# Zero rows under small float32 products, and other rules in the planner that orders the kernel

## The chip, the cores and the metric

One core of a Trainium2 chip runs the whole program in one launch. The metric is the device time of one execution in microseconds (us). A change of about one per cent is the least that a measurement of this kernel can tell from none.

## The reference

Three parts follow each other: a gated recurrence with a matrix state (4 batches, 8 heads, 768 steps, 40 features), then two feed-forward layers on its output (3072 rows of 320).

```python
for t in range(S):
    m_new = np.maximum(f_gate[:, :, t] + m, i_gate[:, :, t])
    f_stab = np.exp(f_gate[:, :, t] + m - m_new)
    i_stab = np.exp(i_gate[:, :, t] - m_new)
    C = f_stab[:, :, None, None] * C + i_stab[:, :, None, None] * np.einsum('bhd,bhe->bhde', vt, kt)
    n = f_stab[:, :, None] * n + i_stab[:, :, None] * kt
    h_tilde = np.einsum('bhde,bhe->bhd', C, qt)
    denom = np.maximum(np.abs(np.einsum('bhd,bhd->bh', n, qt)[:, :, None]), 1.0)
    y[:, :, t] = 1.0 / (1.0 + np.exp(-o_gate[:, :, t])) * h_tilde / denom
...
h = x @ w_in;  x = np.maximum(0.01 * h, h) @ w_out      # layer 0, 320 -> 2048 -> 320
h = np.maximum(x @ w_in, 0.0);  out = h * h @ w_out     # layer 1
```

## The kernel before

The recurrence is done in six chunks of 128 steps. Inside a chunk it has the form of attention: for each of eight groups g (four heads of one batch) the scores of keys and queries (`mS`, line 644, into PSUM tile `attS`), times a decay mask `aw`, times the values (`mPV`, line 660, or `mPV3`, line 666, into `atty`), plus queries times the carried state (`mI`, line 654). The state update is `mU` (line 721), for two batches at a time into `attm`; the outcome is transposed by `mT` (line 763) into `xH` and `xL`, the two halves of the number that the layers multiply. `gate_T` (lines 555, 556) turns the gates of a chunk, `bc` (line 624) spreads them over the partitions in chunk 0.

The first two chunks (`c < NATIVE`) use plain float32 products: their keys and queries lie 40 partitions high in `raw` (tiles `w8` to `w15` in chunk 0, `X` in chunk 1), and the state `C32` is 40 partitions high too. Later chunks stack three copies to 120 partitions (tiles `T`, `Cst`).

Layer 0 and layer 1 split each weight into a high and a low part (`weight`, lines 395 to 421, on VectorE, ScalarE and GpSimd); `moe_h` (line 442) makes a hidden block in `hp` with eight matmuls, `out1` (lines 473 to 479) and `out2` (lines 522 to 524) sum them up in the tiles `acc`. For the first chunk half blocks of 256 columns are used, so that the layer can begin before the whole chunk is there.

No instruction is issued in the order of the code. Each is a `Node` with an engine, an assumed duration in ns, a `key` and what it reads and writes; `Sched.order` runs a planner: `forward` walks through time and gives each free engine the ready node with the least key, `backward` gives each node the latest start that would still do as its next key, six passes, and the shortest plan is issued word for word. When TensorE would have nothing to do, early in the plan, a product of zeros is put in (`sc.idle`; lines 330, 469 and 487, tile `warm`); none of its results is used. A node with `alt` may go to GpSimd in place of VectorE. All transfers are issued on SyncE's queue, in the plan's order. ScalarE's instructions also wait in a row: a change between the tables of Exp and Sigmoid loads a table (ACT_TABLE_LOAD).

Of the kernel before, what the change touches and what calls it, by code (L numbers as in the profile page):

```python
# [19 lines left out]
E = 42  # L20
CH = 128
# [12 lines left out]
PASSES = 6  # L34
WARM = 18500
# [12 lines left out]
class Node:  # L48
    __slots__ = ("eng", "dur", "fn", "key", "deps", "outs", "ndep", "ready", "allocs", "bufs", "end", "start", "table", "lat", "seq", "alt", "after", "first", "bank", "small")


class Sched:
# [10 lines left out]
    def op(self, eng, dur, key, fn, r=(), w=(), table=None, lat=0, alt=None, after=0, small=False):  # L63
# [5 lines left out]
        n.seq, n.outs, n.allocs, n.end = len(self.nodes), [], [], None  # L69
        deps, bufs = {}, {}  # L70
# [25 lines left out]
    def order(self, passes):  # L96


        import copy

        best = None
        for i in range(passes):
            try:
                plan, total = self.forward()
            except RuntimeError:
                if best is None:
                    raise
                break
            if best is None or total < best[1]:
                best = [copy.copy(n) for n in plan], total  # L110
            self.backward(plan, total)
        return best[0]

    def backward(self, plan, total):
# [4 lines left out]
        lst, g = {}, [(-1e9, total)]  # L119
        for n in sorted((n for n in plan if n.seq >= 0), key=lambda n: (n.start, n.seq), reverse=True):  # L120
# [7 lines left out]
            t -= 2000 + n.lat if n.lat else 0  # L128
            if n.eng == "PE":
                i = next(i for i, (lo, hi) in enumerate(g) if min(hi, t) - lo >= n.dur)  # L130
                lo, hi = g[i]
                t = min(hi, t)
                g[i:i + 1] = [x for x in ((t, hi), (lo, t - n.dur)) if x[1] - x[0] > 60]
# [4 lines left out]
    def forward(self):  # L138
        import heapq

# [22 lines left out]
        out, now, dma_free, done, last, small = [], 0.0, 0.0, 0, 0.0, False  # L163
        while done < len(self.nodes):

            for e, cand in ready.items():
# [3 lines left out]
                for n in sorted(cand, key=lambda n: (n.key, n.seq)):  # L170
                    if all(b.live or (b.first is n and queue[b.tag][-1] is b and free[b.tag] > 0) for b in n.bufs):
# [4 lines left out]
                        if e != "PE" or pick.small or not small or n.key > pick.key + STAY:  # L176
                            break
                if pick is None:
                    if e == "PE" and self.idle and (now < 12000 or now - last > 300) and (fill := next((f for f in self.idle if f[1].live and f[2].start is None), None)):
# [4 lines left out]
                        busy[e] = n  # L184
                        heapq.heappush(at, (now + n.dur, 0, -1))
                    continue
                n = pick
                if n.alt:
                    other = n.alt[0] if e == n.eng else n.eng
                    if e != n.eng:  # L190
                        b = busy[other]
                        ahead = (b.start + b.dur - now if b else 0) + sum(x.dur for x in ready[other] if (x.key, x.seq) < (n.key, n.seq) and x.eng == other)
# [3 lines left out]
                    ready[other].remove(n)  # L196
                cand.remove(n)
# [17 lines left out]
                busy[e] = n  # L215
                heapq.heappush(at, (now + dur, 0, n.seq))
                end = now + dur
                if n.lat:
                    begin = max(end + 1300, dma_free)
                    dma_free = begin + n.lat * (1.5 if begin < 13000 else 1.1)  # L220
                    end = dma_free + 700
                n.end = end
# [13 lines left out]
            elif what == 1:  # L236
                ready[n.eng].append(n)
                if n.alt:
                    ready[n.alt[0]].append(n)
# [31 lines left out]
def mlstm_moe_kernel(  # L271
# [40 lines left out]
    C32 = fixed([D, B * H, E], name="C32")  # L312
    Cst = fixed([3 * D, B * H, E], F32R, name="Cst")
    fi, am = sb("x2_0", [32, 2, S]), sb("x2_1", [32, 2, S])
# [19 lines left out]
    def consts():  # L334
        V.memset(mt.t[:, 0:1], NEG)
        V.memset(am.t[:, 1], 1.0)
        V.memset(am.t[:, 1].rearrange("p (k t) -> p k t", t=CH)[:, :, 0:1], 0.0)

    op("DVE", 900, -300, consts, w=[(mt, 0), (am, "mask")])
    op("POOL", 800, -300, lambda: make_identity(nc, ident.t), w=[(ident, 0)])  # L340

    GP = [0, CH, 2 * CH, S]

    def gate_part(lo, hi, key):
# [6 lines left out]
        a = lambda: am.t[:, 0, o]  # L351
# [9 lines left out]
        def clamp():  # L361
            V.tensor_scalar(out=a(), in0=a(), scalar1=AMIN, scalar2=None, op0=ALU.max)
            if lo == 0:
                V.memset(am.t[:, 0, 0:1], 0.0)
# [507 lines left out]
```

## Time and profile before

| | us |
|---|---|
| median of 3 runs | 856.56 |
| lowest and highest | 851.53, 859.89 |
| the profiled execution, its own time | 853.73 |
| its span, first to last instruction | 851.0 |
| mean granted TensorE clock in it | 0.989 |

The profiled execution has 2.73 us outside its span. Its clock is given as a share of 2.4 GHz; 0.50 is 1.2 GHz.

### The profile page before, as it was taken

The page shows a single profiled execution, that of the slowest core. Times are in us where ns is not written, and L with a number is a line of the kernel's source. Part 1 is how long each engine was busy: PE and PEld are TensorE (multiplying, and loading weights), DVE is VectorE, ACT ScalarE, POOL GpSimd, SP SyncE. Part 2 cuts the span into 40 slices and gives each one's busy share as a digit, 9 for nine tenths or more (in the row PEclk, how much of TensorE's full clock was granted, in tenths as well). Part 3 has the DMA queues.
Part 4 walks back from the last instruction along what each step waited for, and adds up shares of the span by engine and source line. Part 5 has one row for each costly group of instructions (what it writes and reads, how often), then busy time and mean ns, then how long its engine had stood idle before and what let it go on. Part 6 is the DMA issues. An engine that isn't in the chain of part 4 may idle for free.

```text
span 851.0 us, 13708 instructions
## 1 busy us (share of the span) xinstructions
PE 836.9 (98%) x5159; PEld 720.7 (85%) x5162; DVE 528.3 (62%) x967; ACT 464.1 (55%) x928; POOL 98.8 (12%) x133
## 2 busy tenths in 40 slices
PE   9899999999999999999999999999999999999998
PEld 6799888788878878887888889999999999999997
DVE  6999955766776786666657898353443533533433
ACT  6678566657766775786455675343433433433332
POOL 2475440202011120001000000000000000000000
PEclk9999989999999999999999999999999999999999
DMA  7677352435344353543322441000000000000000
GB/s 221 225 270 223 99 145 89 138 113 167 109 136 149 127 165 113 167 132 95 99 69 94 146 136 68 1 32 1 1 32 0 24 9 1 32 1 1 32 1 31
DMA packets 52210, 78.58 MB, mean 92 GB/s; under 512 B 4336, under 2 KB 40784, under 8 KB 52144
## 3 DMA queue, kind: packets, MB, share of 16 engines
q1 hardware_dynamic: 52144, 77.71, 28.8%
q8 instruction: 40, 0.66, 0.3%
q14 instruction: 26, 0.21, 0.1%
HBM read 54.26 MB, written 4.01 MB: 68 GB/s over the span
## 4 chain that ended last, share of the span: by engine, by line
PE 75%; DVE 9%; DMA 5%; ACT 4%; SPq 3%; issue 2%; POOL 0%; DVEq 0%; ACTq 0%
PE hp L442 33%; PE acc L473 4%; PE acc L524 3%; PE acc L523 3%; PE acc L522 3%; PE acc L475 3%; PE acc L474 3%; DMA aw<-Adram 3%; SPq L590 3%; PE attS L644 2%; PE acc L478 2%; PE acc L479 2%; PE atty L654 1%; PE atty L524 1%; PE atty L522 1%
## 5 line engine op out<-in xcount | busy, mean ns | idle before, releaser
L442 PE MATMUL hp<-xH,w 128*128 128x512 f32 (+1 forms) x995 | 289.5, 388 | 0.0
L442 PEld LDWEIGHTS hp<-xH,w 128*128 128x128 f32 x995 | 179.4, 189 | 29.8
L442 PE MATMUL hp<-xL,w 128*128 128x512 f32 (+1 forms) x597 | 196.4, 384 | 0.6 <-DVE xL L769 0.6
L454 DVE TENSOR_TENSOR g<-g 128x512 f32<-128x512 f32 x96 | 66.4, 691 | 118.7 <-ACT g L453 118.7
L442 PEld LDWEIGHTS hp<-xL,w 128*128 128x128 f32 x597 | 111.6, 189 | 24.1 <-DVE xL L769 0.8
L453 ACT ACTIVATE g<-hp 128x512 f32<-128x512 f32 x96 | 57.3, 597 | 129.5 <-PE hp L442 129.4
L456 DVE TENSOR_TENSOR gL<-g,gH 128x512 fp32r<-128x512 f32 x96 | 66.4, 692 | 56.4 <-ACT gH L455 56.4
L455 ACT CAST gH<-g 128x512 fp32r<-128x512 f32 x96 | 59.5, 620 | 68.8 <-DVE g L454 68.8
L448 ACT ACTIVATE gH<-hp 128x512 fp32r<-128x512 f32 (+1 forms) x103 | 58.3, 566 | 51.0 <-PE hp L442 46.3
L450 DVE TENSOR_TENSOR gL<-hp,gH 128x512 fp32r<-128x512 f32 (+1 forms) x103 | 66.9, 650 | 30.7 <-ACT hp L449 30.1
L473 PE MATMUL acc<-gH,w 128*128 128x512 f32 (+1 forms) x206 | 82.7, 402 | 0.0
L475 PE MATMUL acc<-gL,w 128*128 128x512 f32 (+1 forms) x206 | 78.3, 380 | 0.0
L474 PE MATMUL acc<-gH,w 128*128 128x512 f32 (+1 forms) x206 | 78.1, 379 | 0.0
L524 PE MATMUL acc<-w,gL 128*128 128x320 f32 x192 | 59.3, 309 | 0.0
L523 PE MATMUL acc<-w,gH 128*128 128x320 f32 x192 | 59.3, 309 | 0.0
L522 PE MATMUL acc<-w,gH 128*128 128x320 f32 x192 | 59.2, 308 | 0.0
L449 ACT ACTIVATE hp<-hp 128x512 f32<-128x512 f32 (+1 forms) x103 | 57.7, 560 | 0.0
L638 POOL TENSOR_SCALAR_AFFINE_SELECT aw<-aw 128x512 f32<-128x512 f32 x48 | 33.6, 701 | 201.6 <-ACT aw L635 172.3
L635 ACT ACTIVATE aw<-aw,cs 128x128 f32<-128x128 f32 x160 | 50.7, 391 | 6.6 <-DMA aw<-Adram 6.3
L475 PEld LDWEIGHTS acc<-gL,w 128*128 128x128 f32 x206 | 39.3, 191 | 7.7 <-DVE gL L450 0.2
L473 PEld LDWEIGHTS acc<-gH,w 128*128 128x128 f32 x206 | 39.6, 192 | 6.3
L474 PEld LDWEIGHTS acc<-gH,w 128*128 128x128 f32 x206 | 39.4, 191 | 5.7
(160 smaller groups left out, 1432.7 us busy)
## 6 DMA issues: line engine op xcount, KB each, us to landing
T<-X SPq DMA_DIRECT2D x144, 120.0 KB
x<-in_wts_dram SPq DMA_DIRECT2D x16, 704.0 KB
aw<-Adram SPq DMA_DIRECT2D x40, 256.0 KB
nat<-in_nat_dram SPq DMA_DIRECT2D x24, 328.0 KB
qkr<-in_qk_dram SPq DMA_DIRECT2D x16, 360.0 KB
X<-in_wts_dram SPq DMA_DIRECT2D x8, 704.0 KB
T<-in_wts_dram SPq DMA_DIRECT2D x8, 704.0 KB
og<-in_og_dram SPq DMA_DIRECT2D x12, 320.0 KB
```

What stands on the lines that cost most here:

```text
L442: T.matmul(hp.t[:, 0:n], w.t[:, col:col + 128], x.t[:, kt, o], start=(s == 0), stop=(s == 7))
L448: op("ACT", act(n, True), key, lambda: A.activation(gH.t[:, 0:n], h(), AF.Prelu, alpha=0.01), r=[(hp, 0)], w=[(gH, 0)])
L450: op("DVE", dve(n), key, lambda: V.tensor_tensor(out=gL.t[:, 0:n], in0=h(), in1=gH.t[:, 0:n].bitcast(F32), op=ALU.subtract), r=[(hp, 0), ( ...
L454: op("DVE", dve(n), key, lambda: V.tensor_tensor(out=g.t, in0=g.t, in1=g.t, op=ALU.mult), r=[(g, 0)], w=[(g, 0)])
L455: op("ACT", act(n), key, lambda: A.copy(gH.t, g.t), r=[(g, 0)], w=[(gH, 0)])
L456: op("DVE", dve(n), key, lambda: V.tensor_tensor(out=gL.t, in0=g.t, in1=gH.t.bitcast(F32), op=ALU.subtract), r=[(g, 0), (gH, 0)], w=[(gL, 0)])
L473: T.matmul(a[t].t[:, o], w.t[:, hc:hc + 128], gH.t[:, 0:n], start=first, stop=False)
L474: T.matmul(a[t].t[:, o], w.t[:, lc:lc + 128], gH.t[:, 0:n], start=False, stop=False)
L475: T.matmul(a[t].t[:, o], w.t[:, hc:hc + 128], gL.t[:, 0:n], start=False, stop=last)
L522: T.matmul(a.t[:, 0:DM], gH.t[:, s], wH, start=first, stop=False)
L523: T.matmul(a.t[:, 0:DM], gH.t[:, s], wL, start=False, stop=False)
L524: T.matmul(a.t[:, 0:DM], gL.t[:, s], wH, start=False, stop=last)
```

## The change

- `pad` writes zeros to partitions 40 to 127 (in two pieces, 64 to 127 and 32 to 63, the transfer or the update writes over 32 to 39 later) of `C32`, of `raw` for groups 4 to 7 in chunk 0, and of `X` once for all of chunk 1. The products `mS` and `mI` of these then run over 128 rows. Groups 0 to 3 of chunk 0 stay at 40 rows. `C32` and `X` are written by ScalarE (four copies), the four tiles of chunk 0 by GpSimd or VectorE (eight memsets).
- Each TensorE node has `act`, the part of its time that counts as activity, weighted by its share of rows. `dense` adds this up over the last `SPAN` of the plan. Where a small product would leave less than `DENSE`, another ready product or a product of zeros goes first.
- A transfer is issued only when fewer than `DEPTH` are in flight in the plan; `backward` places VectorE, ScalarE and the transfers in time too, not TensorE alone; after the six passes 160 rounds change some keys at random and keep what makes the planned time no longer.
- Assumed durations of small products are other numbers (`mS` 248 for 214, `mI` and `mPV` 226, `mU` 850 for 1170, `gate_T` 530 for 380).
- The low part of a weight is made on VectorE by `scalar_tensor_tensor` (times 1, minus) in place of `tensor_tensor`. A second place for products of zeros is opened in chunk 1. The mask of the gates is shorter.

```diff
@@ order
+        rnd = random.Random(3)
+        for i in range(ROUNDS):
+            sigma, mid, half = rnd.choice((300, 1000, 3000)), rnd.uniform(0, 100e3), rnd.choice((5e3, 10e3, 20e3))
+            for n, (k, s) in zip(self.nodes, keys):
+                n.key = k + (rnd.gauss(0, sigma) if abs(s - mid) < half else 0)
...
+            if total <= best[1]:
+                best = [copy.copy(n) for n in plan], total
+                keys = [(n.key, n.start) for n in self.nodes]
@@ backward
-            t -= 2000 + n.lat if n.lat else 0
...
+            if n.lat:
+                t = (place(gaps["DMA"], t - 700, 1.2 * n.lat) if "DMA" in gaps else t - 700) - 1.2 * n.lat - 1300
+            if n.eng in gaps:
+                t = place(gaps[n.eng], t, n.dur)
@@ forward
+        def dense(n):
+            lo = now + n.dur - SPAN
+            while past and past[0][1] <= lo:
+                past.pop(0)
+            return n.act + sum(a * (min(1, (e - lo) / (e - s))) for s, e, a in past) >= DENSE * SPAN
...
+                if e == "PE" and pick is not None and pick.small and 7000 < now and not dense(pick):
+                    other = next((n for _, _, n in cand if not n.small and all(b.live or (b.first is n and queue[b.tag][-1] is b and free[b.tag] > 0) for b in n.bufs)), None)
+                    pick = other or (None if any(f[1].live and f[2].start is None for f in self.idle) else pick)
...
+                if n.lat and len(flight) >= DEPTH:
+                    dur = max(dur, flight[-DEPTH] - now)
@@ the kernel
-    C32 = fixed([D, B * H, E], name="C32")
+    C32 = fixed([128, B * H, E], name="C32")
...
+    def pad(t, buf, n, key, ks, act_=True):
+        for p0, p1 in ((64, 128), (32, 64)):
+            w = [(buf, f"z{p0}")] + (ks if p0 == 32 else [])
+            if act_:
+                op("ACT", act(n), key, lambda p0=p0, p1=p1: A.copy(t()[p0:p1], warm.t[p0:p1, 0:1].to_broadcast([p1 - p0, n])), r=[(warm, 0)], w=w)
+            else:
+                op("POOL", 1.05 * n + 90, key, lambda p0=p0, p1=p1: G.memset(t()[p0:p1], 0.0), w=w, after=5300,
+                   alt=("DVE", dve(n, True), lambda p0=p0, p1=p1: V.memset(t()[p0:p1], 0.0)))
+
+    pad(lambda: C32.t.rearrange("p h e -> p (h e)"), C32, B * H * E, -250, [(C32, (b, k)) for b in range(B) for k in range(2)])
...
+            if eng is V:
+                eng.scalar_tensor_tensor(out=w.t[:, o:o + n], in0=x, scalar=1.0, in1=y, op0=ALU.mult, op1=ALU.subtract)
...
+                    full = c > 0 or g >= 4
+                    if c == 0 or not g:
+                        raw = sb(f"w{(11, 10, 9, 8, 15, 14, 13, 12)[g]}" if c == 0 else "X", [128 if full else D, 2, 4, CH])
+                        if full:
+                            pad(lambda raw=raw: raw.t.rearrange("p a h t -> p (a h t)"), raw, 1024, -240 + g, [(raw, 0)], c > 0)
```

What the change does to the order of instructions is shown at two places. In the rows an operation stands with its line, its tiles and partitions x columns; the line numbers are those of the file that the row is from, and after the change `mS` is line 712, `mI` 722, `mU` 789, `mPV` 728, `mT` 831, `gate_T` 619 and 620, `moe_h` 506, `out1` 537 to 543.

The first is TensorE's row at the last state update of chunk 1 (`mU` into `attm`). Before:

```order
L475 MATMUL acc_235<-gL,w_927 128x512
L721 MATMUL attm<-wv,nat 40x42 x16
L644 MATMUL attS<-X 128x128 x4
L654 MATMUL atty<-C_69,X 128x42 x4
L555 MATMUL attS<-ident,G_sb 128x96
L556 MATMUL attS<-ident,G_sb 128x32
L660 MATMUL atty<-nat,aw 128x42 x4
L478 MATMUL acc_243<-gH,w_927 128x512
```

After:

```order
L728 MATMUL atty<-nat,aw 128x42 x4
L506 MATMUL hp<-xH,w_1039 128x512 x4
L506 MATMUL hp<-xL,w_1039 128x512 x2
L506 MATMUL hp<-xH,w_1039 128x512
L506 MATMUL hp<-xL,w_1039 128x512
L831 MATMUL attm<-ident,y 128x128 x3
L722 MATMUL atty<-C_69,X 128x42 x4
L712 MATMUL attS<-X 128x128 x4
L789 MATMUL attm<-wv,nat 40x42 x16
L728 MATMUL atty<-nat,aw 128x42 x4
L619 MATMUL attS<-ident,G_sb 128x96
L542 MATMUL acc_260<-gH,w_542 128x256
```

The small products still stand in one run here, with a whole hidden block ahead of them; what differs is that the products on `X` and `C32` now have 128 rows each.

The second is ScalarE's row from its start (`og` are the output gates, `d` a one-column tile that only makes a table load early, `cs` and `ex` the turned gates, `aw` the masks of the first groups). Before:

```order
L329 ACT_TABLE_LOAD
L329 ACTIVATE d<-d 128x1
L559 COPY cs<-attS 128x32
L560 ACT_TABLE_LOAD
L560 ACTIVATE ex<-attS 128x96
L635 ACTIVATE aw<-hp,cs 128x128 x4
L635 ACTIVATE aw<-acc_163,cs 128x128 x4
L569 ACT_TABLE_LOAD
L569 ACTIVATE og<-og 128x1280
L635 ACT_TABLE_LOAD
L635 ACTIVATE aw<-acc_194,cs 128x128 x4
```

After:

```order
L395 CAST C_69<-warm 64x1344
L395 CAST C_69<-warm 32x1344
L378 ACT_TABLE_LOAD
L378 ACTIVATE d<-d 128x1
L395 CAST X<-warm 64x1024
L633 ACTIVATE og<-og 128x1280
L395 CAST X<-warm 32x1024
L635 ACT_TABLE_LOAD
L635 ACTIVATE d<-d 128x1
L623 COPY cs<-attS 128x32
L624 ACTIVATE ex<-attS 128x96
L703 ACTIVATE aw<-hp,cs 128x128 x4
```

The four copies of zeros and the Sigmoid of the output gates now stand ahead of the first exponentials, and the table no longer changes between the masks of the first four groups. On SyncE's queue the second part of the gates and the output gates are now issued second and third; before they stood seventh and eighth, behind the first four key and query tiles.

## Rows read from the trace of the kernel before

**Rows 1.** The page, parts 1 and 2: TensorE's busy time, granted clock in 40 slices.

```profile
PE 836.9 (98%) x5159; PEld 720.7 (85%) x5162; DVE 528.3 (62%) x967; ACT 464.1 (55%) x928; POOL 98.8 (12%) x133
...
PEclk9999989999999999999999999999999999999999
```

**Rows 2.** Windows by stage: busy us of each engine, granted clock, DMA share, GB/s.

```profile
0.00:32.38 32.38, 29.52 (x206) 22.09 (x210) 23.31 (x55) 19.21 (x48) 10.26 (x16) 0.95 0.78 236
32.38:105.00 72.62, 70.00 (x561) 62.88 (x561) 70.24 (x127) 52.34 (x121) 42.73 (x54) 0.95 0.60 194
105.00:150.00 45.00, 45.00 (x263) 38.92 (x261) 25.21 (x54) 30.85 (x69) 10.92 (x15) 0.92 0.43 119
150.00:450.00 300.00, 294.65 (x1987) 241.31 (x1987) 204.67 (x424) 195.32 (x412) 34.33 (x48) 1.00 0.40 126
```

**Rows 3.** Windows, the four stretches at the lower clock, columns as in rows 2.

```profile
23.66:27.07 3.41, 3.01 (x33) 2.22 (x35) 2.42 (x8) 0.78 (x2) 0.72 (x1) 0.50 0.82 312
50.96:54.38 3.42, 3.42 (x41) 3.11 (x42) 3.41 (x8) 2.79 (x7) 3.02 (x6) 0.50 0.85 294
78.27:81.68 3.41, 3.41 (x16) 3.31 (x16) 3.30 (x10) 1.75 (x4) 3.25 (x4) 0.50 0.71 176
105.58:112.40 6.82, 6.82 (x28) 6.21 (x28) 4.78 (x11) 5.39 (x16) 5.63 (x8) 0.50 0.29 97
```

**Rows 4.** TensorE's timeline before the fall at 105.58: start, us, instruction, idle before.

```profile
103.39 0.81 PE L721 MATMUL attm<-wv,nat 128*40 128x42 f32 x32 [0.86 <-DVE xL L769]
104.14 1.16 PE L644 MATMUL attS<-X 40*128 40x128 f32 x8
105.13 1.35 PE L654 MATMUL atty<-C,X 40*128 40x42 f32 x8
```

**Rows 5.** TensorE's timeline around small products of 40 and of 128 rows.

```profile
67.87 0.28 PE L474 MATMUL acc<-gH,w 128*128 128x256 f32 x1
67.99 0.28 PE L475 MATMUL acc<-gL,w 128*128 128x256 f32 x1
68.20 1.16 PE L644 MATMUL attS<-X 40*128 40x128 f32 x8
69.19 0.98 PE L654 MATMUL atty<-C,X 40*128 40x42 f32 x8
70.10 0.39 PE L478 MATMUL acc<-gH,w 128*128 128x256 f32 x1
...
71.14 0.98 PE L660 MATMUL atty<-nat,aw 128*128 128x42 f32 x8
71.95 0.47 PE L473 MATMUL acc<-gH,w 128*128 128x512 f32 x1
```

**Rows 6.** ScalarE's timeline at the start.

```profile
8.51 0.19 ACT L559 COPY cs<-attS 128x32 f32<-128x32 f32 x1 [6.22 <-PE attS L556]
8.71 1.28 ACT L560 ACT_TABLE_LOAD   x1
10.01 0.25 ACT L560 ACTIVATE ex<-attS 128x96 f32<-128x96 f32 x1
...
13.64 1.27 ACT L569 ACTIVATE og<-og 128x1280 f32<-128x1280 f32 x1
...
17.41 1.18 ACT L635 ACTIVATE aw<-hp,cs 128x128 f32<-128x128 f32 x4
```

**Rows 7.** VectorE's timeline at the start.

```profile
1.10 0.70 DVE L336 MEMSET x<- 32x768 f32 x1
...
9.31 0.47 DVE L356 TENSOR_TENSOR_SCAN T<-x,T 32x128 f32<-32x128 f32 x1 [3.66 <-DMA x<-in_gates_dram]
```

**Rows 8.** GpSimd's timeline at the start.

```profile
10.34 1.50 POOL L709 TENSOR_TENSOR wv<-nat,ex 128x336 f32<-128x336 f32 x1 [8.96 <-ACT ex L560]
```

**Rows 9.** TensorE's timeline, the products of zeros and the first hidden block.

```profile
1.05 7.00 PE L330 MATMUL hp<-warm 128*128 128x512 bf16 x19 [1.05 <-DVE warm L327]
...
33.67 0.50 PE L442 MATMUL hp<-xL,w 128*128 128x256 f32 x2 [0.56 <-DVE xL L769]
```

**Rows 10.** Groups of instructions with shapes apart: busy us, mean ns, idle before.

```profile
L413 DVE TENSOR_TENSOR w<-x,w 128x512 fp32r<-128x512 f32 x12 | 10.3, 860 | 0.9 <-ACT w L409 0.9
...
L404 DVE SCALAR_TENSOR_TENSOR x<-x,x 128x704 int32<-128x704 int32 x16 | 15.0, 941 | 0.0
```

More of the change, by code (lines that the diff above doesn't have):

```diff
@@ L48 @@
 class Node:
-    __slots__ = ("eng", "dur", "fn", "key", "deps", "outs", "ndep", "ready", "allocs", "bufs", "end", "start", "table", "lat", "seq", "alt", "after", "first", "bank", "small")
+    __slots__ = ("eng", "dur", "fn", "key", "deps", "outs", "ndep", "ready", "allocs", "bufs", "end", "start", "table", "lat", "seq", "alt", "after", "first", "bank", "small", "act")
 class Sched:
@@ L61, in buf, with op @@
         return Buf(tag, make)
-    def op(self, eng, dur, key, fn, r=(), w=(), table=None, lat=0, alt=None, after=0, small=False):
+    def op(self, eng, dur, key, fn, r=(), w=(), table=None, lat=0, alt=None, after=0, small=False, act=None):
         n = Node()
@@ L169, in forward @@
                 pick = None
-                for n in sorted(cand, key=lambda n: (n.key, n.seq)):
-                    if all(b.live or (b.first is n and queue[b.tag][-1] is b and free[b.tag] > 0) for b in n.bufs):
+                for _, _, n in cand:
+                    for b in n.bufs:
+                        if not b.live and (b.first is not n or queue[b.tag][-1] is not b or free[b.tag] <= 0):
+                            break
+                    else:
                         if pick is None:
@@ L177, in forward @@
                             break
+                if e == "PE" and pick is not None and pick.small and 7000 < now and not dense(pick):
+                    other = next((n for _, _, n in cand if not n.small and all(b.live or (b.first is n and queue[b.tag][-1] is b and free[b.tag] > 0) for b in n.bufs)), None)
+                    pick = other or (None if any(f[1].live and f[2].start is None for f in self.idle) else pick)
+                    forced = pick is None
+                else:
+                    forced = False
                 if pick is None:
-                    if e == "PE" and self.idle and (now < 12000 or now - last > 300) and (fill := next((f for f in self.idle if f[1].live and f[2].start is None), None)):
+                    if e == "PE" and self.idle and (forced or now < 12000 or now - last > 300) and (fill := next((f for f in self.idle if f[1].live and f[2].start is None), None)):
                         n = Node()
@@ L191, in forward @@
                         b = busy[other]
-                        ahead = (b.start + b.dur - now if b else 0) + sum(x.dur for x in ready[other] if (x.key, x.seq) < (n.key, n.seq) and x.eng == other)
+                        ahead = (b.start + b.dur - now if b else 0) + sum(x[2].dur for x in ready[other] if x < (n.key, n.seq) and x[2].eng == other)
                         if ahead + n.dur < n.alt[1] * ORDER["bias"]:
@@ L684, in attention @@
                        alt=("POOL", pool(512), lambda lw=lw: lw(G, 1)))
[L685 removed]
+                    op("PE", 4 * 126, key + 0.5, mPV3, small=True, act=420, r=[(pb, (pr, i)) for i in range(3)] + [(vb, (vr, i)) for i in range(3)], w=[(py, 0)])
                 else:
[L687 removed]
+                    op("PE", 4 * 226, key + 0.5, mPV, small=True, act=280, r=[(aw, 0), (nt, 0)], w=[(py, 0)])
                 def comb(py=py, hs=hs, hf=hf, g=g):
```

83 lines of the change are left out of this document (51 added, 32 removed).

## The prediction

> **What bounds the kernel now.** I read the page first: TensorE is busy for 836.9 of 851.0 us, and its granted clock is below full only in the first seventh of the span [rows 1]. So nothing can be won in the second half, and two questions are left: where TensorE waits, and where it runs at half clock. The windows by stage answer the first. Until the first hidden block at 32.38 VectorE is idle for 32.38 - 23.31 = 9.1 us; from there to 105 both engines are nearly full, TensorE 70.00 and VectorE 70.24 of 72.62; from 105 to 150 TensorE is full and VectorE is at 25.21 of 45; from 150 to 450 TensorE loses 300 - 294.65 = 5.35 us in waits [rows 2]. The windows on the clock answer the second: four stretches at 1.2 GHz, 17.06 us together, all before 112.4 [rows 3]. In the last three TensorE was busy all the time (13.65 us), in the first for 3.01 of 3.41, between waits. What stood ahead of the fall at 105.58 is a run of small products: 16 with 40 output partitions, then `mS` and `mI` over 40 of 128 rows [rows 4].
>
> **The change part by part.**
>
> The clock. Work that takes 13.65 us at 1.2 GHz takes half at 2.4, so the last three stretches cost at most 6.8 us, all four at most 8.5. If products over 128 rows keep the clock up where those over 40 did not, that is won; if not, nothing. By the order, the last update of chunk 1 still has all its small products in one run, so there the rows alone must do it. I take 6.8 as the size of it, 3.4 in the stretches at 51 and 78 and 3.4 in that at 105, and leave the first stretch out: TensorE was waiting there.
>
> The Trainium skill, page "TensorE: Matmul & The Clock Gate", section "Why this matters for your kernels", speaks against this: it warns of idle gaps between bursts of matmuls, and part 1 of that page calls the clock gate a monitor of how busy the engine is; rows of the array are not named. By that rule padding could give nothing; I weigh it as a rival below.
>
> Changes between 40 and 128 rows. Two products of 256 columns follow each other after 0.12 us; before an `mS` over 40 rows the same product takes 0.21 (67.99 to 68.20). Eight instructions of `mI` over 40 rows hold TensorE for 0.91 us until the next product starts, eight of `mPV` with the same 42 columns over 128 rows for 0.81 [rows 5]. So going into low rows and coming out cost 0.1 us each. Counted through TensorE's row, there are 42 such changes before and 20 after (groups 0 to 3 of chunk 0 and `gate_T` keep theirs): 22 x 0.1 = 2.2 us, some 2.0 of it between 32 and 105. The rows themselves cost no time: `mS` takes the columns that it has, and nothing is added to TensorE.
>
> The zeros. Four ScalarE copies of 1344 and 1024 columns: by the Sigmoid of 1280 columns in 1.27 us, 2 x 1.33 + 2 x 1.02 = 4.7 us. They lie in the 6.22 us in which ScalarE waits for `gate_T` [rows 6], but that Sigmoid and one more table load (1.27 + 1.28) stand there too now: from 2.3 us the row reaches the exponentials at about 11.3, for 10.01 before. The first mask is 1.3 us later. The fourth, with no table changes between, is done at 11.3 + 0.25 + 4 x 1.18 = 16.3, for 18.6 before: 2.3 us earlier. Of the eight memsets VectorE has four, 0.70 x 1024 / 768 = 0.93 us each, 3.7 together; they fit its wait of 3.66 us for the second part of the gates [rows 7], which is now issued second. GpSimd has the other four and waits 8.96 us there [rows 8]; even at twice VectorE's price they fit. Without that cover each would cost its own length on the way to the first masks.
>
> The start. TensorE's first hidden block waited for VectorE's `xL` [rows 9]. By the new order VectorE has some 5.5 us more work ahead of that `xL` (the memsets, one mask product, parts of weight 1), out of 9.1 us idle. So the block can come up to 3.6 us earlier, or up to 2 us later if the late first mask decides. I take 1 us earlier, nearer to the lower end, since VectorE's new work comes in before its old. Three more products of zeros in all; five more at the very start stand where TensorE had nothing to do, so I take nothing for them.
>
> VectorE as a cap. Between 32 and 105 TensorE can be faster only as far as VectorE is. VectorE can begin this stage earlier by the idle time it no longer has, at most 9.1 - 3.7 = 5.4 us; and the low part of the weights may get cheaper: 860 ns for 512 columns as `tensor_tensor` is 1.68 ns a column, 941 for 704 as `scalar_tensor_tensor` is 1.34 [rows 10]; by the order 11 such instructions remain on VectorE, 11 x 512 x 0.34 = 1.9 us. So of the 3.4 (clock) + 2.0 (row changes) + 1 (start) = 6.4 us between 0 and 6.4 come through; I take 4.5, nearer to the upper end, since 5.4 + 1.9 = 7.3 is above what is asked. In the stage after 105 VectorE is half idle, and the 3.4 us come whole.
>
> From 150 us on the rows of TensorE stand in the same order but for a few places; SyncE's queue has some loads one place earlier or later. I take nothing, and 2 us on either side, from the 5.35 us of waits there.
>
> Sum: 4.5 + 3.4 = 7.9 us. Made against the profiled execution: 853.73 - 7.9 = 845.8, so **846 us**. The median of the runs shown is 856.56, 2.8 above that execution; one per cent of it, 8.6 us, is about what a measurement of this kernel can tell from no change, so below 848.0 counts as faster and above 865.1 as slower.
>
> **The rivals.**
>
> Rows do not count for the clock. Then the falls come as before, since only how busy TensorE is decides. For it: the run of small products at the end of chunk 1 is as long as it was. Against it: the clock fell at 50.96, 78.27 and 105.58 although TensorE was busy for 70.00 of 72.62 us, and the longest wait near the last fall is 0.86 us [rows 2 to 4]. So idleness alone does not explain these falls. (This rival is the rule of the Trainium skill cited above, from "TensorE: Matmul & The Clock Gate".) What is left is the row changes and the start: 853.73 - 2.2 - 1 = 850.5. This is also the case in which the change does not do what it says. Chance 0.17.
>
> VectorE binds fully. The clock stays up, but between 32 and 105 TensorE only waits longer for VectorE, which is at 97 per cent there [rows 2]. Then only the stretch at 105 is won: 853.73 - 3.4 = 850.3. In the profile the waits of TensorE before 105 would grow from 2.6 to about 8 us. Chance 0.16.
>
> ScalarE's row stops at the output gates. Their Sigmoid, now ahead of all masks, waits for a transfer of 640 KB. Its turn comes at about 7.3 us (2.3 + 2.66 + 1.28 + 1.02). For 0.83 MB ahead of and with it, at the 236 GB/s of that stage [rows 2], 3.5 us after the issue are enough, so it should be there by then. Were it to land at 16, all masks would be 8 to 9 us late, with key tiles behind it; VectorE's idle time takes none of that, since it waits for the masks. Then 853.73 + 8.5 - 3.4 = 858.8; with the clock lost as well, 862 to 866. It is slower than before from a landing some 3.5 us after the Sigmoid's turn on. Chance 0.08.
>
> **How the numbers follow.** The forecast has 0.59, with 838 to 849 as its own range: 837.4 if all four stretches (8.5), all changes (2.2), a start 3.6 earlier and 2 us of the later waits are won, 849 if 4.7 of the 7.9 come. Faster by over 1%: 0.59 x 0.92 + 0.05 from the better ends of the first two rivals, 0.59. Slower by over 1%: 0.06, most of it from the third rival at its worst. The same: 0.35. The range that holds 8 in 10 goes from 837 to 857, since the first two rivals lie near 850 and the third only begins at 857.
>
> **What would show it.** Clock: the slices of the page are 9 from the first hidden block on, and no window between 45 and 115 is at 0.50. Row changes: `mI` over 128 rows takes 0.81, not 0.91, until the next product. Start: the first exponentials near 11.5, the fourth mask done near 16, the first hidden block between 29 and 33. VectorE: its share between the first block and the end of the weights' split stays above 0.95, and TensorE's waits there are 2 to 5 us. From chunk 3 of the recurrence on, about 5 us of waits as before. The prediction is wrong if the clock falls at the same places, if TensorE's waits before 105 take up what the clock gives, or if new waits on transfers appear after chunk 2.

## The result and the profile after

| | changed kernel | kernel before, same chips |
|---|---|---|
| median of 12 runs each, us | 860.53 | 853.48 |
| lowest and highest | 856.27, 865.39 | 850.61, 859.89 |
| profiled execution, span, clock | 857.11, 855.4, 0.994 | 853.73, 851.0, 0.989 |

The ratio is 1.0073, with an interval from 1.0046 to 1.0100: slower by 0.7 per cent, on the far side of the forecast of 846 us and above the range. By the bound of one per cent this counts as the same.

In the profiled execution the clock did what was forecast, and the time did not follow. But no other of the 12 executions of the changed kernel has a higher clock: three have 0.994 and took 856.3 to 857.1 us, eight have 0.978 to 0.988 and took 860.0 to 865.4. The median of the 12 is 0.988; that of 114 runs of the kernel before, taken beside the experiments below, is 0.989 (0.978 to 0.996). So over the runs no clock was gained, and what follows is read from one of the best executions. In the page's parts 1 and 2 (a digit of 9 is a mean of 0.9 or more) the clock is now below 9 only in the first slice, before only in the sixth [rows 1]:

```profile
PE 834.8 (98%) x5161; PEld 719.2 (84%) x5165; DVE 536.4 (63%) x974; ACT 467.1 (55%) x931; POOL 101.2 (12%) x134
...
PEclk8999999999999999999999999999999999999999
```

The windows by stage (columns as in [rows 2]), with the two stretches at the lower clock and the last of the old ones:

```profile
0.00:32.38 32.38, 28.11 (x151) 20.44 (x154) 26.07 (x56) 20.45 (x42) 13.73 (x20) 0.89 0.70 217
32.38:105.00 72.62, 67.34 (x556) 61.11 (x557) 71.21 (x124) 54.20 (x129) 38.45 (x46) 0.98 0.59 194
105.00:150.00 45.00, 43.62 (x309) 37.68 (x308) 28.01 (x60) 27.91 (x64) 10.31 (x14) 1.00 0.42 126
150.00:450.00 300.00, 293.59 (x1985) 240.62 (x1984) 204.30 (x422) 195.21 (x413) 37.90 (x53) 1.00 0.40 127
...
12.32:19.14 6.82, 6.82 (x31) 6.37 (x31) 5.11 (x9) 1.98 (x8) 3.02 (x3) 0.50 0.70 202
32.80:36.21 3.41, 3.40 (x43) 3.02 (x42) 3.35 (x7) 2.36 (x9) 1.19 (x1) 0.50 0.31 53
...
105.58:112.40 6.82, 6.34 (x48) 5.74 (x47) 4.73 (x13) 1.64 (x5) 1.31 (x3) 1.00 0.32 88
```

The falls at 51, 78 and 105 us [rows 3] are gone; two new ones stand in the start, 10.2 us together for 17.1 before (the profiled executions). Between 32 and 105 VectorE is at 71.21 of 72.62, and TensorE, slow for 3.4 us there instead of 6.8, waits: its busy time fell from 70.00 to 67.34 while its work came no earlier. TensorE's list of waits up to 105 us (waiting line, releaser, us in total, times, longest) names VectorE:

```profile
PE atty L722 <- DVE hs L767: 1.8, 1, 1.8
PE attm L831 <- DVE y L824: 1.7, 1, 1.7
PE acc L539 <- DVE gL L514: 1.1, 1, 1.1
...
PE attS L619 <- DVE G_sb L431: 1.0, 1, 1.0
PE attS L692 <- DVE aw L715: 0.9, 1, 0.9
```

The loss itself is made in the start. TensorE's timeline (`gate_T` is now line 619, `bc` 692, `mS` 712, `moe_h` 506):

```profile
11.06 0.28 PE L619 MATMUL attS<-ident,G_sb 96*128 96x96 f32 x1 [1.05 <-DVE G_sb L431]
...
11.60 1.45 PE L692 MATMUL acc<-G_sb,ident 96*128 96x128 f32 x8
12.99 2.07 PE L712 MATMUL attS<-w 40*128 40x128 f32 x8
14.99 2.07 PE L692 MATMUL hp<-G_sb,ident 96*128 96x128 f32 x8
...
38.31 0.72 PE L506 MATMUL hp<-xH,w 128*128 128x256 f32 x4
```

The first hidden block comes at 38.31 for 32.38 [rows 2], 5.9 us later. The same product of TensorE is 3.8 us later at 266 us and 4.4 us later at 832, so 1.5 to 2.1 us came back after the start. Of the forecast 7.9 us, 6.9 were to come there. ScalarE and VectorE at the start:

```profile
11.71 0.18 ACT L623 COPY cs<-attS 128x32 f32<-128x32 f32 x1 [0.55 <-PE attS L620]
11.79 0.26 ACT L624 ACTIVATE ex<-attS 128x96 f32<-128x96 f32 x1
17.16 1.14 ACT L703 ACTIVATE aw<-hp,cs 128x128 f32<-128x128 f32 x4 [5.11 <-PE hp L692]
```

```profile
4.01 0.47 DVE L416 TENSOR_TENSOR_SCAN T<-x,T 32x128 f32<-32x128 f32 x1 [0.59 <-DMA x<-in_gates_dram]
...
6.12 0.91 DVE L398 MEMSET w<- 32x1024 f32 x1 [0.27 <-issue]
...
10.63 0.28 DVE L431 TENSOR_TENSOR G_sb<-G_sb,x 32x128 f32<-32x128 f32 x1
11.18 0.91 DVE L398 MEMSET w<- 32x1024 f32 x1 [0.27 <-issue]
...
19.04 0.69 DVE L715 TENSOR_TENSOR aw<-aw,attS 128x512 f32<-128x512 f32 x1 [1.58 <-POOL aw L706]
```

VectorE's wait of 3.66 us for the second part of the gates [rows 7] is no more: that part, issued second, is there at 4.0 us. The four memsets (0.91 us each) stand between the operations on the gates, the first part is done at 10.9, for 5.65 before, and the first mask product starts at 19.04. The exponentials are at 11.79, near the 11.3 of the prediction; but the first mask waits 5.11 us more, since its spread gates come behind an `mS` and another `bc` at half clock.

### The profile page after: what moved, and what is told of

It reads as the page before. It is cut to its first block, busy times and chain, and to the rows that moved or that the text cites. A ratio compares the mean times of both kernels' runs of the same rounds, so it can differ in the third digit from the quotient of the medians.

```text
span 855.4 us, 13715 instructions
## 1 busy us (share of the span) xinstructions
PE 834.8 (98%) x5161; PEld 719.2 (84%) x5165; DVE 536.4 (63%) x974; ACT 467.1 (55%) x931; POOL 101.2 (12%) x134
## 4 chain that ended last, share of the span: by engine, by line
PE 69%; DVE 14%; ACT 6%; DMA 4%; SPq 3%; issue 3%; POOL 0%; ACTq 0%; DVEq 0%
PE hp L506 32%; PE acc L588 3%; PE acc L587 3%; PE acc L586 3%; PE acc L537 3%; DMA aw<-Adram 3%; SPq L654 3%; PE acc L539 3%; PE acc L538 3%; DVE aw L715 2%; PE attS L712 2%; PE acc L542 1%; ACT aw L703 1%; PE acc L543 1%; DVE x L464 1%
## 5 line engine op out<-in xcount | busy, mean ns | idle before, releaser
L506 PEld LDWEIGHTS hp<-xH,w 128*128 128x128 f32 x995 | 178.2, 188 | 30.7 <-DVE gL L514 1.1
L514 DVE TENSOR_TENSOR gL<-hp,gH 128x512 fp32r<-128x512 f32 (+1 forms) x103 | 66.7, 648 | 29.1 <-ACT hp L513 28.3
L537 PE MATMUL acc<-gH,w 128*128 128x512 f32 (+1 forms) x206 | 81.5, 396 | 0.0
L538 PE MATMUL acc<-gH,w 128*128 128x512 f32 (+1 forms) x206 | 77.5, 376 | 0.0
```

The costliest lines, as they stand in the source:

```text
L506: T.matmul(hp.t[:, 0:n], w.t[:, col:col + 128], x.t[:, kt, o], start=(s == 0), stop=(s == 7))
L514: op("DVE", dve(n), key, lambda: V.tensor_tensor(out=gL.t[:, 0:n], in0=h(), in1=gH.t[:, 0:n].bitcast(F32), op=ALU.subtract), r=[(hp, 0), ( ...
L537: T.matmul(a[t].t[:, o], w.t[:, hc:hc + 128], gH.t[:, 0:n], start=first, stop=False)
L538: T.matmul(a[t].t[:, o], w.t[:, lc:lc + 128], gH.t[:, 0:n], start=False, stop=False)
```

## The experiments

Each kernel below issues an order that is written out word for word, so that only what is named moves; `before_...` has the order of the kernel before, `after_...` that of the changed kernel. Times are medians, ratios are to runs of the kernel before on the same chip.

**Rows or busy time: after_rows40.** The changed kernel, its zeros written and not read.

```diff
-lhs = lambda a, h, raw=raw: raw.t[:, a, h % 4]
+lhs = lambda a, h, raw=raw: raw.t[0:D, a, h % 4]
-st = (C32 if native else Cst).t[:, 8 * b + h]
+st = C32.t[0:D, 8 * b + h] if native else Cst.t[:, 8 * b + h]
```

> The order of after, instruction for instruction, zeros written as there, but the products mS and mI of the first two chunks read 40 rows again. Theory A: the clock falls two or three times more between 38 and 115 us, and row changes come back; 4 to 9 us above after (860.5): 865 to 869. Rival B: the falls are as in after (12 and 33 us), only the row changes are dearer, 861 to 863.

Measured: 870.48 us in four runs, ratio 1.0180 (1.0076 to 1.0284), span 865.5 for 855.4. The windows at the lower clock:

```profile
12.13:49.68 37.55, 37.54 (x184) 32.59 (x183) 26.07 (x46) 13.99 (x44) 9.90 (x12) 0.50 0.47 142
63.33:70.16 6.83, 6.83 (x57) 6.48 (x57) 6.83 (x13) 5.54 (x15) 5.08 (x6) 0.50 0.98 336
```

44.4 us at 1.2 GHz for 10.2, with the same instructions in the same order and TensorE busy throughout these windows. Over the runs the mean clock is 0.956 to 0.984, for 0.978 to 0.994 of the changed kernel. A holds in the clock, not in the form: there is one fall behind 38 us, not two or three; the first lasts 30.7 us longer, and the time is above A's range.

**Idle ahead of the first fall: after_busy.** Five more products of zeros ahead of `gate_T`.

```diff
 mS, zeros,
+zeros, zeros, zeros, zeros, zeros,
 gate_T, bc, mS, bc
```

> The order of after with five more products of zeros ahead of gate_T, so that TensorE is not idle from 10.0 to 11.06. gate_T comes no earlier. Theory F (half of the late start is the clock that falls at 12.3 because TensorE stood nearly idle ahead of it): the stretch at 12 us goes or is put off, the first block is 2 to 3.4 us earlier (35 to 36), 857 to 858.5. Rival G (the fall there comes from the small products that follow, of few rows): the clock still falls, 860 to 861.

Measured: 860.15 us, 1.0074 (1.0045 to 1.0102). G: the fall comes a little earlier (10.65) and stays. Three more follow in this execution, at 34.55, 48.20 and 72.09. The last stands behind products over 128 rows and a wait for VectorE (TensorE's timeline, then the window):

```profile
70.41 1.06 PE L817 MATMUL atty<-C,X 128*128 128x42 f32 x8 [1.78 <-DVE hs L862]
```

```profile
72.09:75.50 3.41, 3.41 (x12) 2.73 (x11) 3.41 (x5) 2.12 (x4) 1.40 (x3) 0.50 0.93 270
```

In the profiled execution of the changed kernel the same wait of 1.78 us (at 67.69) is followed by no fall. So 128 rows do not keep the clock up in every execution, and waits may have a part in it; that was not tested apart.

**The memsets of VectorE: after_zeros_gpsimd.**

```diff
-VectorE: memset of partitions 32 to 63 of four key tiles
+GpSimd:  the same four memsets, behind its own four
```

> The order of after with the four memsets of VectorE on GpSimd, else word for word. Theory D (the zeros in VectorE's gate chain make the start late: gate_T at 11.06 for 7.90, then the fall of the clock at 12.3): gate_T at about 9.9, where TensorE's own products of zeros end; no stretch or a shorter one at 12 us; first hidden block at 33 to 36 instead of 38.3; 855 to 858. Rival E (ScalarE's row with the copies and the Sigmoid, or the order of VectorE's gates, sets the start): first block within 1 us of 38.3, 860.

Measured: 854.26 us, 1.0036 (1.0001 to 1.0072), span 852.4. By the spans the memsets cost 3.0 us, by the ratios 0.37 per cent, with intervals that overlap; the medians are 6 us apart, but the clock differs there too (median 0.995 for 0.988). D in direction, the size not settled better than 3 to 6 us. `gate_T` is at 9.93, as D asked; but the falls still stand at 11.42 and 31.90, the first mask product starts at 17.63 and the first hidden block at 37.08, only 1.2 earlier. So there is more to the late start than these memsets.

**The zeros alone: before_zeros.** No instruction of the kernel before moves (only the mask of the gates is the shorter one of the change); the four copies go into ScalarE's 6.22 us of waiting and all eight memsets into GpSimd's 8.96.

```diff
 ScalarE: table load, Sigmoid of one column,
+copy C32, copy C32, copy X, copy X,
 cs, exponentials, masks
 GpSimd: identity,
+memset x 8 (key tiles of groups 4 to 7),
 wv
```

> The order of before, instruction for instruction, with the zeros alone: all eight memsets on GpSimd in its idle time before 10 us, the four copies on ScalarE in its idle time before 8.5 us. Theory A (rows count for the clock, and the loss of the change is its own order): no stretch at 1.2 GHz at 51, 78 and 105 us, changes between 40 and 128 rows mostly gone; 845 to 849 against 853.5 of before. Rival B (rows do not count for the clock): the three stretches stay, only the row changes go, 851 to 853. Rival C (VectorE is the bound between 32 and 105 us, so nothing of it comes through there): the stretches at 51 and 78 go, waits take their place, 849 to 851.

Measured: 853.61 us, 1.0001 (0.9972 to 1.0030): no difference that these runs can tell, with the clock at 0.996 and no fall behind 28.3 us. A and C have the clock, B is out; the time lies above the ranges of all three. How much earlier (-) or later (+) the same VectorE operations stand than in the trace of before, in us, read at six places of it; the later experiments with this order are here too:

```
place in before (us)    39.7   81.9  117.6  250.0  448.0  836.2
before_zeros             1.6    1.9   -0.3   -1.1   -0.0    1.3
before_zeros_warm       -0.7    0.2   -1.7   -3.2   -2.0   -0.7
before_zeros_light      -2.8   -4.5   -8.1   -7.6   -6.4   -5.1
before_light             1.2    0.6   -0.3   -1.7   -1.7   -1.7
before_zeros_pool       -0.7   -0.3   -2.5   -3.9   -2.2   -0.8
before_zeros_x          -0.6   -0.2   -1.5   -3.1   -2.5   -2.6
before_zeros_dve        -1.2   -1.8   -3.0   -4.0   -3.1   -3.1
before_dve_rows40       -1.4    0.1    0.3    0.6    1.1    1.1
```

From 39.7 to 81.9 the row of VectorE keeps its distance to the trace of before, although TensorE was at half clock there for two stretches in the one and at full clock in the other. In this pair of executions the clock's gain shows only between 81.9 and 117.6 us, where the last stretch of before lies: 2.2 us. And the start is 1.6 us late: the first fall now lasts from 21.43 to 28.26 (6.8 us for 3.4), and VectorE waits 1.78 us for it.

**Relieving VectorE: before_zeros_light and before_light.**

```diff
-V.tensor_tensor(out=ft(), in0=ft(), in1=l.t, op=ALU.add)
+n = WR - 352 * (layer == 0)
+V.tensor_tensor(out=ft()[:, 0:n], in0=ft()[:, 0:n], in1=l.t[:, 0:n], op=ALU.add)
```

> The order of before with the zeros (as before_zeros, 853.6 us), and VectorE relieved: the step that adds the low bits to the rebuilt float32 weights is done for 352 of 704 columns in each tile of the first layer, so the low bits of the other columns are left out. That takes some 12 x 0.5 = 6 us from VectorE between the first hidden block and 85 us. Theory V (with the clock up, VectorE's row sets the end of the stretch from about 26 to 82 us, and what the clock gave is waited away there): the time falls to 847.5 to 850.5 us, since TensorE was busy for only 66.0 of 72.6 us there. Theory U (something else holds the stretch, such as transfers or ScalarE): 852.5 to 854.5 us.

> The kernel before without zeros, with the same relief of VectorE (the low bits of half of the columns of the first layer's weights left out). Theory V: TensorE was busy for 70.0 of 72.6 us there because its clock fell, so at most 2.6 us can be won: 850.5 to 852.5 us, 2 to 4 us above before_zeros_light; that difference is what the clock is worth once VectorE leaves room for it. Theory U: 853 to 854 us, the same as with the zeros.

Measured: 849.86 us, 0.9981 (0.9948 to 1.0014), span 846.0; and 851.08 us, 0.9953 (0.9924 to 0.9982), span 849.3. Both medians lie where V put them, but V wanted them 2 to 4 us apart, and they are 1.2. By its ratio the relief alone is a gain clear of noise, some 4 us (1.5 to 6.5), where V allowed at most 2.6. In the profiled executions the two parts need each other: at 117.6 us the zeros alone gave 0.3 us, the relief alone 0.3, both 8.1. The windows from 32.38 to 105, first with and then without zeros, show that at half clock TensorE had no room (72.06 of 72.62).

```profile
32.38:105.00 72.62, 69.22 (x589) 63.15 (x587) 67.78 (x135) 57.10 (x136) 47.66 (x57) 1.00 0.63 206
```

```profile
32.38:105.00 72.62, 72.06 (x569) 65.28 (x571) 63.72 (x125) 53.88 (x126) 44.70 (x55) 0.93 0.62 203
```

Over all runs the two cannot be told apart (the ratios overlap, and stand the other way round); runs of before_zeros_light go from 844.5 to 855.8, those of before_light from 844.3 to 853.2. The three fastest of before_light (844.3 to 847.0) have a clock of 0.997 or 0.998, without a zero row: its profiled execution, at 0.988, is not one of them. So it is shown that VectorE's work counts; that the clock is worth nothing without the relief is not.

**VectorE in the changed kernel: after_light.** The same edit there.

> The changed kernel with VectorE relieved as in before_zeros_light (the low bits of 352 of 704 columns of each first-layer weight tile left out), some 7 us less work on VectorE before 105 us. Theory V (in the changed kernel too VectorE's row sets the end of the first 100 us, so what is added to or taken from that row comes through): 852 to 856 us, from 860.2. Rival S (the late start and the fall of the clock at 12.3 us set it, by TensorE's row): 858 to 861 us.

Measured: 852.39 us, 0.9994 (0.9959 to 1.0029), against 1.0073 (1.0046 to 1.0100) of the changed kernel: 0.8 per cent, the intervals apart. V. The falls stand where they stood (12.29 to 19.11, 32.77 to 36.18), so it is VectorE's work, not the clock, that came through. The runs at a clock of 0.994 agree: 850.5 to 852.8 us, for 856.3 to 857.1 of the changed kernel.

**The fall at 21 us: before_zeros_warm.**

```diff
 bc,
+zeros, zeros,
 mPV, mS, mS, zeros, zeros, zeros, zeros, mPV,
+zeros, zeros, zeros, zeros,
 zeros, bc
```

> As before_zeros (853.6 us), with six more products of zeros on TensorE where it waited: two at 13.3 us and four at 18.6 us. Theory W (the fall of the clock from 21.4 to 28.3 us makes the first xL, and with it VectorE's row, 1.6 us late, and this is what the rest of the gain went to): the fall goes or is shorter, the first hidden block comes 1.5 to 2.5 us earlier than in before_zeros, and the time is 851 to 852.5 us. Rival N (the fall comes all the same, or the start has slack): 853 to 854.5 us.

Measured: 852.12 us, 0.9995 (0.9977 to 1.0013). The fall at 21 us goes and the first hidden block is at 31.21 for 33.65, as W has it; but another fall comes at 48.15 to 54.98 and takes 1 us back (line two of the table). In the time it can't be told from before_zeros.

**The gates first: after_gate_first.**

```diff
 VectorE of the changed kernel:
-first and second part of the gates in turn, memsets between
+first part whole, memset x 4, second part, third part
```

> The changed kernel (860.2 us) with VectorE's row at the start in another order: all operations on the first part of the gates first, then the four memsets of zeros, still on VectorE, then the second part. Theory D (the memsets and the second part stood in the chain to the first gates, and that made the start late): the first part is done near 6 instead of 10.9 us, the fall of the clock at 12.3 us is shorter or later, the first hidden block comes 2 to 5 us earlier, 855 to 858 us. Rival K (it is the 3.7 us of work on VectorE, wherever it stands, or the transfers of key tiles that wait for the zeros): 859 to 861 us.

Measured: 859.99 us, 1.0095 (1.0063 to 1.0127), span 864.5. D is refuted as I put it. The first part is done at 5.8, the first mask starts at 13.78 instead of 17.16; but VectorE's row still holds the other parts ahead of the first mask product (18.49 for 19.04), TensorE waits for it, and the clock is at half from 18.06 to 38.54, and again from 48.78, 76.09 and 246.75 (0.980 over the span, the lowest of its ten runs; the median is 0.988). VectorE, then TensorE:

```profile
17.12 1.11 DVE L522 TENSOR_TENSOR x<-x,T 32x512 f32<-32x512 f32 x1
18.16 0.41 DVE L517 TENSOR_SCALAR x<-x 32x512 f32<-32x512 f32 x1
18.49 0.67 DVE L810 TENSOR_TENSOR aw<-aw,attS 128x512 f32<-128x512 f32 x1
```

```profile
16.00 0.38 PE L628 MATMUL acc<-warm 128*128 128x512 bf16 x1
19.22 2.07 PE L807 MATMUL attS<-w 40*128 40x128 f32 x8 [2.83 <-DVE aw L810]
```

**The memsets where VectorE waits: before_zeros_dve.**

```diff
 VectorE of before_zeros: first part of the gates,
+memset x 4 (taken from GpSimd),
 second part, mask product, mask product, third part
```

> As before_zeros (order of before, zeros), but four of the eight memsets of the key tiles stand on VectorE, behind the first part of the gates and ahead of the second, where VectorE waits 3.7 to 4.6 us for that part's transfer in this order (the first of these key tiles is fetched one place later). Theory C (a memset on VectorE is free where VectorE waits; the changed kernel paid for it since its second part is there early and the wait is gone): within 1 us of before_zeros, 852.5 to 854.5 us. Rival P (such memsets cost their 4 us or more wherever they stand on VectorE): 857 to 860 us.

Measured: 850.52 us, 0.9962 (0.9932 to 0.9992), span 847.8, clock 1.000. P is out. The time is 2.0 us below C's range, which C does not explain; what C says of the memsets holds: VectorE's timeline shows that they fill the wait, and the second part starts when its transfer lands.

```profile
6.10 0.91 DVE L492 MEMSET w<- 32x1024 f32 x1 [0.27 <-issue]
...
9.32 0.91 DVE L492 MEMSET w<- 32x1024 f32 x1 [0.16 <-issue]
10.42 0.53 DVE L511 TENSOR_TENSOR_SCAN T<-x,T 32x128 f32<-32x128 f32 x1 [0.18 <-DMA x<-in_gates_dram]
...
12.75 0.65 DVE L810 TENSOR_TENSOR aw<-aw,attS 128x512 f32<-128x512 f32 x1
```

The same four memsets as in the changed kernel, and the first mask product is at 12.75.

**What the rows are worth there: before_dve_rows40.** The kernel above with the edit of after_rows40.

> before_zeros_dve (850.5 us, no stretch at half clock in its profile) word for word, with the zeros written, but the products read the 40 rows with data. Theory A (the rows of the products are what keeps the clock up there): stretches at 1.2 GHz near 21 to 28, 51 and 78 us or 105 us come back, and the time is 852.5 to 855.5 us, so the rows are worth 2 to 5 us. Rival B (the gain of before_zeros_dve is the start's, from the shorter gate mask and the copies, and has nothing to do with rows): 850 to 851.5 us.

Measured: 853.62 us, 0.9988 (0.9964 to 1.0012), span 852.1 for 847.8. Windows of this kernel, then the first of them in before_zeros_dve:

```profile
48.57:55.39 6.82, 6.82 (x58) 6.43 (x57) 6.81 (x12) 5.31 (x16) 4.91 (x7) 0.50 0.76 196
92.94:96.35 3.41, 3.41 (x14) 3.02 (x14) 3.38 (x9) 0.80 (x3) 0.00 (x0) 0.50 0.50 129
106.59:113.42 6.83, 6.83 (x25) 6.19 (x26) 5.26 (x12) 4.58 (x15) 6.06 (x8) 0.50 0.41 115
```

```profile
48.57:55.39 6.82, 6.68 (x82) 6.33 (x80) 6.82 (x12) 5.74 (x17) 5.08 (x7) 1.00 0.86 270
```

A by the clock: 17.1 us at half clock come back in the profile, and over twelve runs of each the clock is 0.982 to 0.994 for 0.993 to 1.000. The longest wait of TensorE in the 8 us ahead of the fall at 48.57 is 0.6 us; before_zeros_dve waits 0.9 us there and stays at full clock. In the span it is 4.2 us; by the ratios the rows are worth 0.26 per cent, with intervals that overlap.

**Without chunk 0's zeros: before_zeros_x.**

```diff
-full = c > 0 or g >= 4
+full = c > 0
```

> As before_zeros, but chunk 0 is left at 40 rows: no memsets, only the four copies of zeros on ScalarE, for C32 and for the key tiles of chunks 1 and 2. Theory S (chunk 0's zeros only moved the first fall of the clock and held back transfers): first hidden block at 32 to 33 us instead of 33.65, 851 to 853 us. Rival R (chunk 0's zeros keep up the clock before 32 us and at 51 us): a stretch at 1.2 GHz comes back near 51 us, 854 to 856 us.

Measured: 850.25 us, 0.9950 (0.9926 to 0.9974). S, a little better than it asked: first hidden block at 32.28, one stretch at half clock at 24.17, near the first of before, none at 51 or 105, one new at 92.44. Chunk 0's eight memsets buy nothing. With before_zeros_dve this beats both kernels; the two can't be told apart.

**Low parts to GpSimd: before_zeros_pool.**

```diff
 before_zeros_warm, weight tiles 2, 6 and 8 of layer 0
-op VectorE: low(V, 768, 512, 0)
+op GpSimd:  low(G, 768, 512, 0)
```

> As before_zeros_warm (852.1 us), with three low parts of weight tiles (512 columns) moved from VectorE to GpSimd, between 35 and 85 us. Theory V: VectorE has some 2.7 us less in the stretch that it sets, and the time is 849.5 to 851 us. Rival G (GpSimd's longer operation, 1.3 to 1.5 us, comes too late for TensorE, or slows VectorE beside it): 852 to 854 us.

Measured: 852.77 us, 0.9984 (0.9959 to 1.0009). Rival G by the time. TensorE now waits 1.3 us once for a low part of GpSimd's; in the table the profile stands 0.8 us ahead of before_zeros_warm at 117.6, and 0.1 at the end.

**The start of one with the rest of the other: after_start.**

```diff
 all engines of the changed kernel
-the first 19 us (to bc of the fifth mask)
+the first 19 us of before_zeros_dve, what was drawn in ahead of them right behind
```

> The changed kernel's order, except that the first 19 us (up to TensorE's product for the fifth mask) stand on all engines as in before_zeros_dve: the first masks ahead of the output gates' Sigmoid on ScalarE, the memsets on VectorE behind the first part of the gates, and the second part's later operations behind the first mask products. The loads and operations that the changed kernel had drawn into that stretch come right behind it. Theory O (the loss of the changed kernel is the order of its first 20 us on VectorE and ScalarE): the first mask product at 13 to 14 instead of 19.0 us, the first hidden block 3 us or more earlier than its 38.3, 850 to 854 us. Rival Q (the rest of the changed order loses it, in the waits on VectorE between 32 and 105 us): 857 to 861 us.

Measured: 856.14 us, 1.0019 (0.9997 to 1.0040), against 1.0073 (1.0046 to 1.0100): 0.54 per cent, the intervals apart. The first mask product is at 12.84, yet the first hidden block only at 37.62:

```profile
37.62 0.72 PE L601 MATMUL hp<-xH,w 128*128 128x256 f32 x4
```

```profile
22.83:36.48 13.65, 11.46 (x73) 9.78 (x74) 10.90 (x23) 4.95 (x14) 3.00 (x4) 0.50 0.62 210
```

The time lies between the ranges of O and Q, and each is half right: about half of the 1.1 per cent between the changed kernel and before_zeros_dve is made in the first 19 us. The trace says where the rest begins: VectorE makes the low part of a weight tile (27.22, 1.77 us) ahead of the first output `y` at 28.91, TensorE waits 1.4 us for that `y`, and its clock is at half. That this order costs the rest was read, not tried.

## Why the prediction was wrong

The step that failed is the start. The sum had it at 1 us earlier and left the clock of this stretch out. In the profiled execution the first hidden block came 5.9 us later, with 10.2 us at half clock up to 36.2 us, where the kernel before had 3.4; and after_start shows that the order of the first 19 us costs 0.54 per cent, about half of what parts the changed kernel from before_zeros_dve.

- **The zeros: a cover that was gone.** The prediction covered VectorE's four memsets by "its wait of 3.66 us for the second part of the gates", and added that this part "is now issued second". A part that is issued second is not waited for: VectorE had it at 4.0. The cover was read from the row of before, for an order in which it no longer was. Without it each memset was to "cost its own length on the way to the first masks": four with their gaps are 4.6 us; 3.0 us of span were measured (after_zeros_gpsimd), and no cost where the wait is real (before_zeros_dve). It is a part of the loss only: without these memsets the first hidden block still came at 37.08.
- **The start: the same error once more.** "1 us earlier" came from 5.5 us more work against 9.1 us idle, as amounts. What counts here is the place: the added operations stood ahead of the first mask product (19.04 for 12.55), and the idle time was elsewhere. The first hidden block was 5.9 us late, far outside the bounds of 3.6 earlier to 2 later. The falls at 12.3 and 32.8 us, which the prediction didn't look for, lie in this part; leaving the first stretch out should have had a bound on the side of a loss too.
- **VectorE as a cap: mis-sized.** 4.5 of 6.4 us were to come through. In the profiled execution of before_zeros, where nothing else moves, VectorE's row gained nothing from 39.7 to 81.9 us, and after_light shows that what is taken from VectorE comes back in the time. This is the second rival, which had 0.16; its price, only the stretch at 105, is near what before_zeros shows there (2.2 us, forecast 3.4). How much of the clock VectorE holds back stays open: of 35 runs of the kernel before beside before_zeros_dve, the 15 with a clock up to 0.988 have a median of 855.9 us, the 14 from 0.992 on one of 850.5. Their mean clocks differ by 0.0073, which is some 6.2 us of TensorE's time (an estimate, 0.0073 x 854), so most of it came through there; at which stretches, no trace shows. And before_zeros_dve and before_zeros_x beat the kernel before with no relief of VectorE. One reason given for the larger share falls too: the low part is no cheaper as `scalar_tensor_tensor`. Per-column prices of two shapes and two operations were set against each other [rows 10]; the same shape has the same price, and 512 columns are now 948 for 860. Groups of before, then of after:

```profile
L413 DVE TENSOR_TENSOR w<-qkr,w 128x576 fp32r<-128x576 f32 x16 | 12.4, 774 | 0.2
```

```profile
L475 DVE SCALAR_TENSOR_TENSOR w<-qkr,w 128x576 fp32r<-128x576 f32 x16 | 12.4, 774 | 0.2
L475 DVE SCALAR_TENSOR_TENSOR w<-x,w 128x512 fp32r<-128x512 f32 x11 | 10.4, 948 | 0.0
```

- **The clock: right in the mechanism, not in the amount.** The falls at 51, 78 and 105 went in the profiled execution, and rows count (after_rows40, before_dve_rows40); the first rival is out. But the 6.8 us were not won over the runs (median 0.988 for 0.989): in the profile new falls in the start take back more than half of what the rows gave, and after_busy and after_gate_first, with the same zeros, fell again at 48 and at 72 or 76. By the Trainium skill, page "TensorE: Matmul & The Clock Gate", section "Why this matters for your kernels", idle gaps would decide; the kernels with 40 rows do not agree with that as the whole rule: TensorE was busy for 37.54 of 37.55 us at half clock in one, and for all of 17.06 in the other.
- **Row changes: right in the row**; what they gave in the time no run tells apart. `mI` over 128 rows holds TensorE for 0.81 us (79.18 to 79.99), as reckoned.
- **ScalarE's row: right up to the exponentials.** The output gates' Sigmoid ran at 7.32, as reckoned, without a wait; the third rival didn't occur. But the first mask, put at 1.3 us later, came 7.0 later (17.16 for 10.16). From 150 to 450 us TensorE lost 6.4 us in waits for 5.35, within the 2 us allowed.

## What to carry to other kernels

A wait covers new work only if it is still there in the new order, and only ahead of the instruction that waits: lay each added instruction into the engine's new row and follow that row to the first result that another engine wants; total idle time is no cover. Where two engines are both nearly full, a gain on one may not come through: take work from each apart and from both before it is counted. Here the zeros alone gave nothing in one placement (before_zeros) and 0.4 and 0.5 per cent in two others (before_zeros_dve, before_zeros_x); the relief of VectorE alone gave 0.5 per cent (before_light). Look at the clock of all runs before a profile is explained, since a single execution can be one of the best. And small products of few rows can pull TensorE's clock down while it is nearly always busy; zero rows raise it, if they are written in time that is really free, but falls remain in some orders.

## What the runs showed of the hardware

Rows count: the same products over 128 instead of 40 rows kept the clock at 1.00 where it fell to 0.50 (before_zeros_dve and before_dve_rows40, the same order; 0.993 to 1.000 against 0.982 to 0.994 over the runs). They are not all that counts: with 128 rows the clock fell at 72.09 in after_busy and not in the changed kernel, at the same products.

The falls differ between executions of one kernel, and the time goes with them: the kernel before had a clock of 0.978 to 0.996 in 114 runs, the changed kernel 0.978 to 0.994 in 12.

In four kernels (before_zeros, and with _light, _warm and _pool) the last stage, in which TensorE is full, is 1.3 to 1.4 us longer than in before, with the same instructions: the table's last two columns; before_light and before_zeros_dve have no such loss. The four have all eight memsets on GpSimd in the order of before. after_zeros_gpsimd has them there too and no loss, so the memsets by themselves are not the cause; it stays open.
